# Where the third batch's quad 1 gets its norms: in the attention of the batch before, or amid the GELUs of the second w_in stage

## The chip, the cores and the metric

The kernel runs on one core of a Trainium2 chip. The metric is the device time of one execution in microseconds (us); "time" below is the median of several executions. A core has five engines that run in parallel, each strictly through its own list of instructions: TensorE (PE) multiplies matrices, ScalarE (ACT) evaluates functions such as exp and GELU, VectorE (DVE) and GpSimd (POOL) do elementwise work and sums, and SyncE (SP) issues transfers. They wait for each other through semaphores. PE writes its results to PSUM, [...]and an engine has to read a bank out before PE may write it again.

## The reference

Two steps in a row. First an attention with cosine scores over 8 batches of 12 heads, 448 positions and head dimension 64:

```python
q_n = q / (np.linalg.norm(q, axis=-1, keepdims=True) + 1e-06)
k_n = k / (np.linalg.norm(k, axis=-1, keepdims=True) + 1e-06)
scores = np.matmul(q_n, k_n.transpose(0, 1, 3, 2)) / tau
attn = softmax(scores)                     # max subtracted, exp, divided by the sum
attn_out = np.matmul(attn, v)
```

Then a feed-forward layer on x, the attention's output laid out as 3584 tokens of 768: `gelu_exact(x @ w_in) @ w_out`, with w_in 768 x 2048 and w_out 2048 x 768. Every row of q and k needs the root of its sum of squares before any score can be made; these norms are what the change is about.

## The kernel before

**Units of work.** Four heads make a quad; a batch has three quads, the kernel 24. A unit is a quad (quad 0 of the whole kernel is split into units 0 and 1), so quad g is unit g+1: the second batch (b = 1) has units 4, 5, 6, the third batch (b = 2) units 7, 8, 9, the fourth begins with unit 10.

**The norms of a unit** take this chain: `load_qk` (SP; q and k, 448 KB each), `square` (POOL, L156, 128x1792), `reduce` (DVE, L165, the sum of squares), `logs` (ACT, Ln, L172), `roots` (ACT, Exp of half the logarithm, L181), `inverses` (POOL adds 1e-6, L190; DVE reciprocal, L192), `scale` (POOL, twice, L208, writes bf16), `transposes` (SP, a transposing transfer, L220). `groups` says which units share one call of the three middle steps (`logs`, `roots`, `inverses`); the third batch's units 7 and 8 form one group, units 9 and 10 the next.

**The attention of a quad**: `scores` (PE, L246) into a pair of PSUM banks, `exps` (ACT, L253) from there, seven passes per quad; `both` then makes the row sums (PE, L275, tile `sm`), turns and inverts them on DVE (L297 to L318), multiplies by the values (PE, L289) and normalises (DVE, L323) into x.

**The stages.** For each batch b: `attention(b, fill)`, then `first(b)`, the w_in stage. The second matrix product (w_out, L352) of earlier tokens is cut into single matmuls, the list `fill`, that are dealt out between the attention's passes by `run()`; after each 16 of them DVE copies the finished bank out (tile `ot`, L356). A w_in stage is 16 blocks m of six matmuls each (L655), every block followed by one GELU on ACT (L691). ACT holds one table of functions at a time: a table load (L647, L693, L695, L700) comes before GELUs and before exps or logarithms.

**PSUM.** Two single banks, `mm0` and `mm1`, are handed out in turn by `mm_tile`; the row sums take the one whose turn it is. Three pairs, `st0`, `st1`, `st2`, serve scores and values. In `first(b)` with b of 1 or more,

```python
pairs = {2: 0, 4: 1} if b else {0: 1, 2: 0, 6: 1, 8: 0}
ahead = 6 if b else 5
```

so blocks 2 and 3 lie in `st0`, blocks 4 and 5 in `st1`, and blocks 0, 1, 6, 7, 8, ... 15 alternate over the two single banks: block 6 takes block 0's bank, block 7 takes block 1's, block 8 takes block 6's. In the first stage (b = 0) blocks 0, 1, 6, 7 lie in `st1`, blocks 2, 3, 8, 9 in `st0`, and the single banks hold blocks 4, 5 and then 10 to 15. The first `ahead` blocks are begun with four of their six matmuls, and finished with the last two once x is complete.

**The order** of every engine's list is the order of the calls in the program (a manual schedule). `upto(f, n)` calls step f for all units before n that have not had it. The first w_in stage already has a break amid its GELUs: after block 5 it loads the exp table, takes the roots of group 5 (units 5 and 6) and loads the GELU table again (L692 to L698).

Of the kernel before, what the change touches and what calls it, by code (L numbers as in the profile page):

```python
# [16 lines left out]
def kernel(  # L17
# [20 lines left out]
    NQ = H // 4  # L38
# [60 lines left out]
    def mm_tile(name, shape=(128, 512), dtype=F32, aside=None):  # L99
        t = ps_mm.tile(list(shape), dtype, tag=f"mm{turn[0] if aside is None else turn[0] ^ aside}", name=name)  # L100
        if aside is None:
            turn[0] ^= 1
        return t

    def pair(i, name):
        pool = third[0] if i == 2 else ps_st
        return pool.tile([128, 2, 512], F32, tag=f"st{i}", name=name)
# [3 lines left out]

    units = [(0, 0, 1), (0, 1, 2)] + [(g, 0, 2) for g in range(1, NG)]
    NU = len(units)
    groups = [[n] for n in range(NQ + 2)] + [[NQ + 2, NQ + 3], [2 * NQ + 1, 2 * NQ + 2]]
    for n in range(3 * NQ, NU, NQ):
        groups += [[n, n + 1], [n + 2]] if n + 2 < NU else [[n]]
    shapes = [[len(gr), 2, units[gr[0]][2] - units[gr[0]][1], C] for gr in groups]
# [51 lines left out]
    def logs(n):  # L169
        nq = nq_t.pop(n)  # L170
        ln_t[n] = nrm.tile(list(nq.shape), F32, tag="lq", name=f"lq{n}")
        nc.scalar.activation(ln_t[n], nq, AF.Ln, bias=tiny)  # L172

    def roots(n):
        ln = ln_t.pop(n)
        if n <= NQ:
            sr_t[n] = root2[n % len(root2)][:, :math.prod(shapes[n])]
            nc.scalar.activation(sr_t[n][:, :, 0], ln.rearrange("p j i s c -> p (j i s c)"), AF.Exp, scale=0.5)
        else:
            sr_t[n] = nrm.tile(list(ln.shape), F32, tag="sr", name=f"sr{n}")  # L180
            nc.scalar.activation(sr_t[n], ln, AF.Exp, scale=0.5)  # L181

    def inverses(n):
        sr = sr_t.pop(n)
        shape = [128] + shapes[n]
        se = nrm.tile(shape, F32, tag="se", name=f"se{n}")
        if n <= NQ:
            nc.vector.tensor_reduce(se.rearrange("p j i s c -> p (j i s c)"), sr, mybir.AxisListType.X, ALU.add)
        else:
            nc.gpsimd.tensor_scalar(se, sr, 1e-6, None, ALU.add)  # L190
        rn = nrm.tile(shape, F32, tag="rn", name=f"rn{n}")
        nc.vector.reciprocal(rn, se)  # L192
        rn_t[n] = rn
# [20 lines left out]
    def transposes(u, i=None):  # L214
        g, s0, s1 = units[u]
        qkb = qkb_t[g]
        if g not in qkT_t:
            qkT_t[g] = qkTp.tile([128, 2, C, 128], BF16, tag="qkT", name=f"qkT{g}")
        if i is None:
            nc.sync.dma_start_transpose(out=qkT_t[g].rearrange("p i c s -> p (i c) s"),  # L220
                                        in_=qkb.rearrange("p i c s d -> p (i c s d)"))
            return
        tp = tp_t[u, i] = mm_tile(f"tp{u}_{i}", (128, C, 128), BF16)
        for c in range(C):
            nc.tensor.transpose(tp[64 * s0:64 * s1, c, :], qkb[:, i, c, s0:s1].rearrange("p s d -> p (s d)"), ident)  # L225

    def copies(u, i):
        g, s0, s1 = units[u]
        rows = slice(64 * s0, 64 * s1)
        nc.vector.tensor_copy(qkT_t[g][rows, i], tp_t.pop((u, i))[rows])  # L230
# [94 lines left out]
    def both(g, p):  # L325
        sums(g)
        turned(g)
        inverted(g)
        spread(g, 0)
        spread(g, 1)  # L330
        values(g, p=p)
        normalise(g, 0)
        normalise(g, 1)
# [64 lines left out]
    def upto(f, n, last=None):  # L398
        last = {load_qk: NG, load_v: NV, root: len(groups), load_wi: 4, load_wo: 4}.get(f, NU)
        while done.get(f, 0) < min(n, last):  # L400
            done[f] = done.get(f, 0) + 1
            f(done[f] - 1)
# [180 lines left out]
    def visit(b, pairs):  # L583
        for p in pairs:
            n, c = passes[at.get(b, 0)]
            at[b] = at.get(b, 0) + 1
            scores(b * NQ + n, ((0, c), (1, c)), p)
            exps(b * NQ + n, ((0, c), (1, c)))

    def attention(b, fill):  # L590
        fill = list(fill)
        if len(fill) == 128:
            parts = iter((20, 18, 20, 22, 32, 16))
        else:
            parts = iter((20, 13, 14, 17, 16, 16) if b == 1 else (16, 14, 16, 18, 16, 16))

        def run():
            for _ in range(next(parts)):
                fill.pop(0)()

        x_t[b] = xp.tile([128, KD, S], BF16, tag="x", name=f"x{b}")
        g0, u = b * NQ, b * NQ + 1
        run()
        upto(scale, u + 3)
        upto(transposes, u + 3)
        if b == 1:
            upto(load_qk, g0 + NQ + 2)
            upto(square, u + 4)
        visit(b, (0, 1, 2))
        if b > 1:  # L610
            upto(scale, u + 4)
            upto(transposes, u + 4)
        run()
        visit(b, (0, 1, 2))
        run()
        upto(load_qk, g0 + NQ + 3)
        visit(b, (0, 1) if b <= 2 else (0, 1, 2))
        upto(reduce, u + 4)
        upto(square, u + 5)
        run()  # L620
        visit(b, (0, 1, 2))
        both(g0, 0)
        upto(load_v, b + 3)
        upto(load_qk, g0 + NQ + 4)
        visit(b, (1, 2))
        upto(reduce, u + 5)
        run()
        visit(b, (1, 2, 0))
        both(g0 + 1, 1)
        visit(b, (2, 0))  # L630
        n = 2 * b + 4
        if n < len(groups):
            logs(n)
            roots(n)
        run()
        both(g0 + 2, 2)
        if n < len(groups):
            inverses(n)
            done[root] = n + 1
            if b > 1:  # L640
                visit(b + 1, (0, 1))

    def first(b):
        sb, hf = divmod(b, 2)
        if hf == 0:
            g_t[sb] = gp.tile([128, KF, 2 * S], BF16, tag="g", name=f"g{sb}")
        nc.scalar.preload_act_table_set(GELU_SET)  # L647
        u = (b + 1) * NQ + 1
        hps = {}
        pairs = {2: 0, 4: 1} if b else {0: 1, 2: 0, 6: 1, 8: 0}  # L650
        ahead = 6 if b else 5

        def mm(m, kds):
            for kd in kds:
                nc.tensor.matmul(hps[m], lhsT=wi[:, kd, m * 128:(m + 1) * 128],  # L655
                                 rhs=x_t[b][:, kd, :], start=(kd == 0), stop=(kd == KD - 1))

        def bank(m):
            if m in pairs:
                st = pair(pairs[m], f"hp{b}_{m}")  # L660
                hps[m], hps[m + 1] = st[:, 0, :S], st[:, 1, :S]
            elif m not in hps:
                hps[m] = mm_tile(f"hp{b}_{m}")[:, :S]

        for m in range(ahead):
            bank(m)
            mm(m, range(KD - 2))
        if b == 0:
            upto(square, u + 3)
            upto(scale, u + 1)  # L670
            upto(transposes, u + 1)
            upto(load_wo, 4)
            upto(reduce, u + 3)
        else:
            upto(scale, u + 2)
            upto(transposes, u + 2)
            upto(load_qk, (b + 1) * NQ + 5)
            upto(square, u + 4)
            upto(reduce, u + 4)
        for m in range(ahead):  # L680
            mm(m, range(KD - 2, KD))
        for m in range(KF):
            if b == 0 and m == 8:
                for i in range(2):
                    transposes(4, i)
                    copies(4, i)
            if m >= ahead and (m == 0 or m - 1 not in pairs):
                for k in range(m, m + 1 + (m in pairs)):
                    bank(k)
                    mm(k, range(KD))  # L690
            nc.scalar.activation(g_t[sb][:, m, hf * S:(hf + 1) * S], hps.pop(m), AF.Gelu)  # L691
            if b == 0 and m == 5:  # L692
                nc.scalar.preload_act_table_set(EXP_SET)  # L693
                upto(root, 6)
                nc.scalar.preload_act_table_set(GELU_SET)  # L695
                upto(scale, u + 2)
                upto(transposes, u + 2)
                upto(load_qk, 2 * NQ + 1)  # L698
        if b + 1 < B:
            nc.scalar.preload_act_table_set(EXP_SET)  # L700
            if b <= 1:
                visit(b + 1, (0, 1, 2))
            upto(root, 2 * b + 6)

    upto(load_qk, 1)
    nc.scalar.preload_act_table_set(EXP_SET)
# [3 lines left out]
    late = nrm.tile([128, 1], F32, tag="late", name="late", bufs=1)  # L710
# [56 lines left out]
```

## Time and profile before

| what | value |
|---|---|
| median of 5 runs | 415.63 us (415.43 to 415.67) |
| the profiled execution: its time / its span | 415.63 us / 413.9 us |
| busy share of the span: PE, ACT, DVE, POOL | 98%, 59%, 46%, 40% |
| second attention, b = 1 (PE) | 52.1 to 80.7 us |
| second w_in stage, b = 1 (PE) | 80.7 to 99.0 us |
| third attention, b = 2 (PE) | 99.0 to 132.4 us |

The span is what the profiler saw from first to last instruction; 1.7 us of the execution's time lie around it. A line of the timeline gives the start, the duration, the engine, the line of the kernel, the operation, output and inputs, and in brackets how long the engine had been idle and who released it. A line of the chain gives the start, the duration, and the engine and tile of one piece of the work that ended last. "x5" counts instructions that the answer merged.

### The profile page before, as it was taken

Reading aid. Unit: us, or ns where it says so; the run is one execution under the profiler, and the core shown is the slowest. Engines: PE = TensorE matmul, PEld = TensorE weight load, DVE = VectorE, ACT = ScalarE, POOL = GpSimd, SP = SyncE. Lnnn points to the kernel's source line nnn. Section 1 sums busy time; section 2 is a strip of 40 time slices with the busy share of each in tenths; the row PEclk is TensorE's granted clock in tenths of the full one; section 3 lists DMA queues with packets and bytes.
Section 4 is the critical chain, followed back from the end, with each engine's and each line's share of the span. In section 5 each row is a group of like instructions: output and inputs, shape, how many; then the busy total and the mean of one; then the engine's idle time right before and its main releaser. Section 6 shows DMA issues by size and latency. Waiting matters only on the chain.

```text
span 413.9 us, 8268 instructions
## 1 busy us (share of the span) xinstructions
PE 406.9 (98%) x3506; PEld 212.4 (51%) x3506; DVE 188.4 (46%) x379; ACT 246.1 (59%) x358; POOL 166.9 (40%) x113
## 2 busy tenths in 40 slices
PE   7999999999999999999999999999999999999996
PEld 3445554555555555555555555555555555555564
DVE  5787216913278222943148431783118711481021
ACT  6895695546646567754764658755665467754300
POOL 4999706083810919044630537217370233000000
PEclk9999999999999999999999999999999999999999
DMA  8999998834396405935296332965088120510033
GB/s 290 261 261 206 204 227 274 185 66 115 62 226 200 122 13 91 280 93 123 25 209 216 66 107 46 219 188 133 2 171 190 40 44 2 120 40 2 0 78 77
DMA packets 66996, 54.53 MB, mean 132 GB/s; under 512 B 38672, under 2 KB 62352, under 8 KB 66960
## 3 DMA queue, kind: packets, MB, share of 16 engines
q1 hardware_dynamic: 54464, 41.79, 39.1%
q0 software_dynamic: 12112, 11.80, 18.1%
q8 instruction: 27, 0.44, 0.4%
q10 hardware_dynamic: 384, 0.43, 0.3%
q14 instruction: 9, 0.07, 0.1%
HBM read 45.61 MB, written 11.01 MB: 137 GB/s over the span
## 4 chain that ended last, share of the span: by engine, by line
PE 94%; DMA 2%; ACT 1%; DVE 1%; POOL 1%; issue 0%; SPq 0%; POOLq 0%
PE hp L655 35%; PE op L352 32%; PE st L246 9%; PE o L289 8%; PE sm L275 4%; PE spin L407 2%; DMA qk<-in_k_dram 2%; PE op L371 1%; PE sm L266 1%; PE tp L225 1%; ACT pt L253 1%; POOL sq L156 1%; DVE nq L165 0%; DVE qkT L230 0%; ACT g L691 0%
## 5 line engine op out<-in xcount | busy, mean ns | idle before, releaser
L253 ACT ACTIVATE pt<-st 128x896 bf16<-128x896 f32 x168 | 142.9, 917 | 67.2 <-PE st L246 66.9
L352 PE MATMUL op<-wo,g 128*128 128x384 bf16 x864 | 147.8, 326 | 0.0
L655 PE MATMUL hp<-x,wi 128*128 128x448 bf16 x768 | 146.8, 353 | 0.0
L352 PEld LDWEIGHTS <-g 128*128 128x128 bf16 x864 | 81.5, 98 | 62.3 <-issue 10.9
L655 PEld LDWEIGHTS <-wi 128*128 128x128 bf16 x768 | 74.4, 98 | 71.4 <-issue 2.9
L691 ACT ACTIVATE g<-hp 128x448 bf16<-128x448 f32 x128 | 65.9, 545 | 70.8 <-PE hp L655 70.5
L208 POOL TENSOR_TENSOR qkb<-qk,rn 128x896 bf16<-128x896 f32 (+1 forms) x49 | 79.6, 1649 | 40.5 <-DVE rn L192 40.5
L165 DVE TENSOR_REDUCE nq<-sq 128x28 f32<-128x1792 f32 (+2 forms) x30 | 48.8, 1637 | 58.0 <-POOL sq L156 55.3
L356 DVE COPY ot<-op 128x384 f32<-128x384 f32 x54 | 29.5, 548 | 95.5 <-PE op L352 93.4
L156 POOL TENSOR_TENSOR sq<-qk 128x1792 f32<-128x1792 f32 (+1 forms) x22 | 66.5, 3035 | 13.3 <-DMA qk<-in_k_dram 13.3
L190 POOL TENSOR_SCALAR se<-sr 128x28 f32<-128x28 f32 (+1 forms) x14 | 4.3, 309 | 125.5 <-ACT sr L181 125.4
L246 PE MATMUL st<-qkT 64*64 64x448 bf16 x672 | 47.8, 358 | 0.2 <-DVE qkT L230 0.2
L289 PE MATMUL o<-pt,v 64*64 64x448 bf16 x672 | 36.9, 352 | 0.0
L246 PEld LDWEIGHTS <-qkT 64*64 64x64 bf16 x672 | 18.3, 105 | 23.8 <-issue 15.4
L318 DVE STREAM_TRANSPOSE rs<-rc 128x448 f32<-128x448 f32 x48 | 28.1, 623 | 0.8
L323 DVE TENSOR_TENSOR x<-o,rs 128x448 bf16<-128x448 f32 x48 | 27.0, 599 | 1.0 <-DVE rs L318 0.5
L192 DVE RECIPROCAL rn<-se 128x28 f32<-128x28 f32 (+2 forms) x18 | 6.8, 376 | 43.4 <-POOL se L190 43.2
L289 PEld LDWEIGHTS <-v 64*64 64x64 bf16 x672 | 17.7, 106 | 16.9 <-issue 8.4
L297 DVE STREAM_TRANSPOSE tr<-sm 128x448 f32<-128x448 f32 x24 | 15.5, 647 | 13.8 <-PE sm L275 10.7
L275 PE MATMUL sm<-pt,ones 128*32 128x448 bf16 (+1 forms) x336 | 17.8, 332 | 0.7 <-DVE ot L356 0.7
L309 DVE TENSOR_REDUCE tr<-tr 32x28 f32<-32x28 f32 x84 | 16.5, 196 | 1.6
L407 PE MATMUL spin<-blank,ident 128*128 128x448 bf16 x34 | 10.3, 449 | 2.2 <-DVE root L89 1.9
(43 smaller groups left out, 115.5 us busy)
## 6 DMA issues: line engine op xcount, KB each, us to landing
qk<-in_q_dram SPq DMA_DIRECT2D x23, 448.0 KB, 6.2
qk<-in_k_dram SPq DMA_DIRECT2D x23, 448.0 KB, 8.6
out_dram<-ot SPq DMA_DIRECT2D x48, 192.0 KB, 3.4
v<-in_v_dram POOLq DMA_DIRECT2D x7, 672.0 KB, 12.4
wi<-in_moe_w_in_dram POOLq DMA_DIRECT2D x8, 384.0 KB, 13.3
wo<-in_moe_w_out_dram POOLq DMA_DIRECT2D x4, 768.0 KB, 13.7
out_dram<-ot SPq DMA_DIRECT2D x12, 96.0 KB, 2.2
qk<-in_q_dram SPq DMA_DIRECT2D x2, 224.0 KB, 3.4
```

The costliest lines, as they stand in the source:

```text
L156: eng.tensor_tensor(sq[:, part], t[:, part], t[:, part], ALU.mult)
L165: nc.vector.tensor_reduce(nq[:, part], sq[:, part], mybir.AxisListType.X, ALU.add)
L208: eng.tensor_tensor(qkb[:, i, :, s0:s1].rearrange("p c s d -> p s c d"), t[:, i, s0:s1], rn[:, i].to_broadcast([128, s1 - s0, C, D]), ALU. ...
L246: nc.tensor.matmul(st[cols, n, :S], lhsT=qkT[rows, 1, c, cols], rhs=qkT[rows, 0, :, cols], start=True, stop=True, tile_position=(64 * s, 6 ...
L253: nc.scalar.activation(pt[:, :m], st[:, :m, :S], AF.Exp, scale=inv_tau)
L275: nc.tensor.matmul(bank_t[g, "sm"][r:r + 32, cols], lhsT=ones, rhs=pt_t[g, s, c][:, cols], start=(c < 2), stop=(c >= C - 2), tile_position ...
L289: nc.tensor.matmul(bank_t[g, h][cols, :S], lhsT=v_t[g][rows, s, c, :], rhs=pt_t[g, s, c][rows], start=(c == 0), stop=(c == C - 1), tile_po ...
L318: nc.vector.transpose(rs, bank_t[g, "rc"][:, h].to_broadcast([128, NB, 32]))
L352: nc.tensor.matmul(ps[:, :NH], lhsT=g_t[sb][:, kf, t * 128:(t + 1) * 128], rhs=wo[:, kf, ni * NH:(ni + 1) * NH], start=(kf == 0), stop=(kf ...
L356: nc.vector.tensor_copy(ot[:, ni * NH:(ni + 1) * NH], ps[:, :NH])
L655: nc.tensor.matmul(hps[m], lhsT=wi[:, kd, m * 128:(m + 1) * 128], rhs=x_t[b][:, kd, :], start=(kd == 0), stop=(kd == KD - 1))
L691: nc.scalar.activation(g_t[sb][:, m, hf * S:(hf + 1) * S], hps.pop(m), AF.Gelu)
```

## The change

All of it is about the third batch's units 7 and 8 (quads 0 and 1), in the second attention and the second w_in stage.

- Units 7 and 8 each become a group of their own; the later groups' numbers move up by one, which the new `(b > 1)` and `(b > 0)` terms follow.
- In `attention(1)` the sum of squares of unit 7 moves from between the second `run()`s to after `both(g0, 0)`, that is behind the normalisation of quad 0 of the second batch, where the sum of unit 8 stood. The sum of unit 8 leaves the attention.
- At the end of `attention(1)`, `logs`, `roots` and `inverses` take unit 7 alone.
- In `first(1)`, ahead of the last two matmuls of the opening blocks, only unit 7 is scaled and transposed, only unit 9 is squared, and the sum of unit 8 stands there.
- In `first(1)`, after the GELU of block 5: exp table, roots of unit 8, GELU table, then scale and transpose of unit 8, square of unit 10 and the sums of units 9 and 10.

```diff
-    groups = [[n] for n in range(NQ + 2)] + [[NQ + 2, NQ + 3], [2 * NQ + 1, 2 * NQ + 2]]
+    groups = [[n] for n in range(NQ + 2)] + [[NQ + 2, NQ + 3], [2 * NQ + 1], [2 * NQ + 2]]
...
         visit(b, (0, 1) if b <= 2 else (0, 1, 2))
-        upto(reduce, u + 4)
         upto(square, u + 5)
...
         visit(b, (1, 2))
-        upto(reduce, u + 5)
+        upto(reduce, u + 4 + (b > 1))
...
-        n = 2 * b + 4
+        n = 2 * b + 4 + (b > 1)
...
-            upto(scale, u + 2)
-            upto(transposes, u + 2)
+            late = int(b == 1)
+            upto(scale, u + 2 - late)
+            upto(transposes, u + 2 - late)
             upto(load_qk, (b + 1) * NQ + 5)
-            upto(square, u + 4)
-            upto(reduce, u + 4)
+            upto(square, u + 4 - late)
+            upto(reduce, u + 4 - 2 * late)
...
-            if b == 0 and m == 5:
+            if b <= 1 and m == 5:
                 nc.scalar.preload_act_table_set(EXP_SET)
-                upto(root, 6)
+                upto(root, 6 if b == 0 else 8)
                 nc.scalar.preload_act_table_set(GELU_SET)
                 upto(scale, u + 2)
                 upto(transposes, u + 2)
-                upto(load_qk, 2 * NQ + 1)
+                if b == 0:
+                    upto(load_qk, 2 * NQ + 1)
+                else:
+                    upto(square, u + 4)
+                    upto(reduce, u + 4)
...
-            upto(root, 2 * b + 6)
+            upto(root, 2 * b + 6 + (b > 0))
```

## The prediction

> **What bounds the kernel now.** I read the page's busy shares first, then the chain that ended last in order of time, then the waits of PE, and then the timelines of the two places that the diff touches. The busy shares:
>
> ```profile
> PE 406.9 (98%) x3506; PEld 212.4 (51%) x3506; DVE 188.4 (46%) x379; ACT 246.1 (59%) x358; POOL 166.9 (40%) x113
> ```
>
> PE is the bound, so only what opens or closes a gap on PE counts. The chain shows one stretch after the start in which PE does not carry it:
>
> ```profile
> 52.17 0.55 ACT g L691
> 52.88 8.32 DMA qk<-in_k_dram
> 61.32 3.18 POOL sq L156
> 64.53 2.02 DVE nq L165
> 66.55 0.48 DVE ot L356
> 67.07 0.85 PE sm L275 x16
> ...
> 80.78 18.27 PE hp L655 x96
> ```
>
> From 67.07 to the copy that closes the run at 410 every piece is PE. The waits of PE between 30 and 110 us are a single entry:
>
> ```profile
> PE sm L275 <- DVE ot L356: 0.7, 1, 0.7
> ```
>
> The timeline there:
>
> ```profile
> 64.53 2.02 DVE L165 TENSOR_REDUCE nq<-sq 128x28 f32<-128x1792 f32 x1 [4.88 <-POOL sq L156]
> 65.59 0.76 PE L246 MATMUL st<-qkT 64*64 64x448 bf16 x12
> 66.47 1.01 DVE L356 COPY ot<-op 128x384 f32<-128x384 f32 x2
> 67.07 0.85 PE L275 MATMUL sm<-pt,ones 128*32 128x448 bf16 x16 [0.71 <-DVE ot L356]
> ```
>
> The sum of squares of unit 7 stands at the head of DVE's list from about 59.7 and waits 4.88 us for POOL's square, which waited for k to land. Behind it is queued the copy that empties the single bank the row sums want. Both copies run at 66.47 and PE has stood for 0.71 us. That gap is all that the first part of the change can win.
>
> The second place is the w_in stages. First stage, ACT, where the break amid the GELUs is already there:
>
> ```profile
> 37.77 2.81 ACT L691 ACTIVATE g<-hp 128x448 bf16<-128x448 f32 x6 [4.06 <-PE hp L655]
> 40.60 1.28 ACT L693 ACT_TABLE_LOAD   x1
> 42.07 0.34 ACT L172 ACTIVATE lq<-nq,tiny 128x56 f32<-128x56 f32 x1 [0.19 <-DVE nq L165]
> 42.45 0.25 ACT L181 ACTIVATE sr<-lq 128x56 f32<-128x56 f32 x1
> 42.71 1.28 ACT L695 ACT_TABLE_LOAD   x1
> 44.01 0.98 ACT L691 ACTIVATE g<-hp 128x448 bf16<-128x448 f32 x2
> ```
>
> From the end of the GELU of block 5 (37.77 + 2.81 = 40.58) to the start of block 6's GELU (44.01) the break takes 3.43 us, 0.19 of it a wait for DVE: 3.24 us without. PE has no wait in that stage. Second stage, PE and ACT, without a break:
>
> ```profile
> 80.71 18.33 PE L655 MATMUL hp<-x,wi 128*128 128x448 bf16 x96
> 86.97 2.43 ACT L691 ACTIVATE g<-hp 128x448 bf16<-128x448 f32 x5 [0.16 <-PE hp L655]
> 88.26 1.15 ACT L691 ACTIVATE g<-hp 128x448 bf16<-128x448 f32 x2
> 90.00 0.54 ACT L691 ACTIVATE g<-hp 128x448 bf16<-128x448 f32 x1 [0.59 <-PE hp L655]
> ```
>
> The second line holds blocks 2 to 6; the third is an answer for a narrower window and holds blocks 5 and 6. One GELU takes 0.54, so block 5's runs 88.26 to 88.80 and block 6's 88.87 to 89.41. The 96 matmuls start 0.189 apart (the first at 80.71, the last at 98.7: 18.0/95), so block 8, the 49th, starts at 80.71 + 48 x 0.189 = 89.8.
>
> **What the Trainium skill says.** (1) "ScalarE: Activation LUTs", section "What ACT_TABLE_LOAD costs", gives about 1283 ns for the load plus about 1380 ns of drain, about 2.66 us for a switch. The trace has the 1.28, and then the next instruction within 0.02 us (42.71 + 1.28 = 43.99, GELU at 44.01): no drain of that size here. I price with the trace; the skill's two switches would be 5.3 us. (2) Same page, section "Table sets: the hidden batching unit": logarithm and exp share a set, GELU has its own, so the break costs two loads, as the first stage shows. (3) "TensorE: Matmul & The Clock Gate", section "Part 1: The HAM clock gate": after one idle window of about 3.4 us the PE clock halves, and it takes one such window of work to come back. No run here shows it: the longest gap of PE in the middle is 0.71 us and the clock row of the page stands at 9 in all 40 slices.
>
> **The change, part by part.**
>
> *Unit 7's sum behind the normalisation.* The copy of the bank (its last matmul ends at about 63.0) no longer queues behind a stalled instruction and is over by 63.6; the row sums start when the scores leave PE, at 66.36. Next late is the third scores pair of the pass after: its exps end at 66.03 + 2.54 = 68.57, and PE would be there at about 68.5, so some 0.04 us stay (in the third attention the same place takes 0.42 us, here 0.38). Gain 0.71 - 0.04 = 0.67 us. DVE in the stretch 69.4 to 80.7 is busy 10.95 of 11.3 us, but it gets no second sum: unit 7's 2.0 us take the place of unit 8's 2.00 us at 72.25, with its square long done (64.5). Were the gain nil, because something else holds the row sums: 0; it cannot exceed 0.71.
>
> *Unit 8's sum in the w_in stage.* DVE is idle from 84.1 to 94.1 there; 2.0 us from 83.9 hide and end at 86, before the logarithm at 89. The copies of the later attention start at 104. Cost 0. Unit 7's logarithm, root, add and reciprocal at half width are 0.02 to 0.2 us shorter each, hidden as well.
>
> *The break in the second stage (times before the 0.67 shift).* ACT: block 5's GELU ends 88.80; load to 90.10; logarithm of 28 columns 0.32 and root 0.23, from start to start 0.35 to 0.41 (their pairs at 31.84/32.19 and 128.64/129.05), so the root ends at about 90.74; load to 92.03; block 6's GELU 92.05 to 92.59. Together 3.2 us in the place of 0.06. Queued behind it: the GELUs of 6 and 7. Who waits: block 8, which takes block 6's single bank and would start at 89.80. It starts 0.04 after the GELU's end, at 92.6. Stall on PE: 92.6 - 89.8 = 2.8 us. In the first stage the same break is free because blocks 6 to 9 lie in two pairs that blocks 0 to 3 have left, and the single banks come back only for block 10; in the second stage only blocks 6 and 7 have banks. The slack was 89.80 - 89.41 = 0.4 us; the break is eight times that. After it block 9 needs the GELU of 7 (ends by 93.1, PE wants it at 93.8) and block 10 that of 8, as before: no second stall. Bounds: 2.7 (shortest spacing) to 3.0 (a wait as the 0.19 above); the skill's drain would make it 4.9, which the trace excludes.
>
> *What moves on POOL, SP and DVE.* POOL: scale of unit 7 (2 x 1.66) from about 84, square of unit 9 (3.15) to 90.5, the add for unit 8 at about 91, its scale to 95, square of unit 10 to 98. DVE: reciprocal of unit 8 between, sums of 9 and 10 to 100.5 instead of 99.2; their logarithm was at 103.34 and goes to about 105.5 by the stall. SP: one transpose (about 2.4), then the load of quad 10, now some 3 us earlier, then unit 8's transpose behind the wait for its scale, about 95 to 98; nothing but stores and loads of the next attention is behind it, and those come after 103. Its result is first needed by scores at 106.86. Cover some 9 us; cost 0. Without cover it would be PE waiting by as much as it is late.
>
> *Sum.* -0.67 + 2.8 = +2.1 us on the profiled span: 413.9 to 416.0, and that execution's time 415.63, equal to the median of the runs, to 417.7. PE has no idle after 67.07 that could swallow the delay, so all of it reaches the end.
>
> **Rivals.**
>
> *A, the gain alone (other side).* The break hides as in the first stage, 415.63 - 0.67 = 414.96. This needs block 8 to have a bank other than block 6's, or the break to be shorter than 0.4 us; the kernel breaks even at a break of 0.4 + 0.67 = 1.1 us, and one table load alone is 1.28. For: the first stage does it without a wait. Against: the bank order in the second stage, which the diff leaves.
>
> *B, the clock.* PE stands 2.8 us, and the gate halves its clock for about one window: estimate from the skill's 3.4 us, half of it lost, +1.7: 419.4. Against: 2.8 is under the window. For: the margin is small and the trace shows no gap like it. From 3.4 us of idling it decides.
>
> *C, the gap at 66.4 stays* (the row sums held by exps or another copy): 415.63 + 2.8 = 418.4. Against: the exps of quad 3's passes are long done there, and the batch after has no gap in that place.
>
> *D, stalls partly met*: block 8's stall about half as large, because ACT's break starts earlier or overlaps, 416.4; or a further 0.5 to 1 us when block 9 or 10 waits again, 418.5.
>
> **How the numbers follow.** Main case 0.74 (417.3 to 418.2), A 0.05, B 0.09, C 0.05, D 0.07. Main, C and most of D give over 0.8 between 416.8 and 419.0; I take that as the range. Chances, with 0.2% (0.83 us) as about what a measurement of this kernel can tell from no change: faster only in A, and there 0.67 is just short of the bound, so 0.03; within 0.2%: the rest of A and a sliver of D, 0.04; slower 0.93.
>
> **What would show it.** Right: no wait of PE on an `ot` copy near 66.4; two further table loads at about 88; one wait of PE on ACT's GELU, 2.8 us long, in the second w_in stage at about 89.1; that stage 21.1 us long instead of 18.3; every later stage as long as before. Wrong: no wait there (A), matmuls spaced wider than 0.19 after it (B), a wait left near 66.4 (C).

## The result, and the profile after

The changed kernel takes 419.21 us (median of 43 executions, 417.34 to 421.63) against 415.66 us (median of 80) before. Compared side by side the ratio is 1.0077, 95% interval 1.0067 to 1.0086: slower by 2.8 to 3.6 us.

The profiled execution has a span of 416.9 us, 3.0 more than before. It began its first w_in stage at 32.53 us instead of 33.09, 0.56 us sooner in a part that the change leaves alone: at the start the matmuls are 0.373 us apart up to 5.59 us in this trace, up to 7.37 us in that of the kernel before, and 0.189 us from there on, so this execution came to its full speed earlier. Its second w_in stage began 1.27 us sooner (79.44 instead of 80.71) and is 4.31 us longer; together that is the 3.0. The medians lie 3.55 us apart (419.21 - 415.66).

The waits of PE in the changed kernel, columns as before (total us, times, longest):

```profile
PE hp L654 <- ACT g L691: 2.7, 1, 2.7
```

The wait of the row sums on the copy `ot` is gone from the list, and this one is new. The timeline where the old wait was:

```profile
62.58 0.56 DVE L356 COPY ot<-op 128x384 f32<-128x384 f32 x1 [3.49 <-PE op L352]
65.18 0.56 DVE L356 COPY ot<-op 128x384 f32<-128x384 f32 x1 [2.04 <-PE op L352]
65.77 0.85 PE L275 MATMUL sm<-pt,ones 128*32 128x448 bf16 x16
...
70.96 2.00 DVE L165 TENSOR_REDUCE nq<-sq 128x28 f32<-128x1792 f32 x1
```

The two copies run when their matmuls end, the row sums start without a bracket (no wait), and unit 7's sum runs behind the normalisation. In the chain the row sums start at 65.84 instead of 67.07; 0.56 of these 1.23 us is the earlier start, and the other 0.67 is the gain over an execution that starts like the profiled one of the kernel before. (With the sum in its old place an earlier start would not have brought the row sums forward: they wait for a transfer there, as experiment 4 shows.)

The second w_in stage, ACT and PE:

```profile
85.71 1.85 ACT L691 ACTIVATE g<-hp 128x448 bf16<-128x448 f32 x4 [0.16 <-PE hp L654]
87.58 1.28 ACT L693 ACT_TABLE_LOAD   x1
88.87 0.32 ACT L172 ACTIVATE lq<-nq,tiny 128x28 f32<-128x28 f32 x1
89.28 0.23 ACT L181 ACTIVATE sr<-lq 128x28 f32<-128x28 f32 x1
89.53 1.28 ACT L695 ACT_TABLE_LOAD   x1
90.82 0.98 ACT L691 ACTIVATE g<-hp 128x448 bf16<-128x448 f32 x2
91.42 10.66 PE L654 MATMUL hp<-x,wi 128*128 128x448 bf16 x48 [2.72 <-ACT g L691]
```

Block 5's GELU ends at 87.56, block 6's starts at 90.82: a break of 3.26 us. Block 8 starts 0.05 us after block 6's GELU (90.82 + 0.55 = 91.37). And the 48 matmuls from block 8 on take 10.66 us; the same 48 take 9.24 at full clock (experiment 1 below). The table by stretch says why. Its columns are the stretch, its length, busy us (and instructions) of PE, PE's weight loads, DVE, ACT and POOL, then the granted PE clock, the DMA share and GB/s:

```profile
79.44:88.70 9.26, 9.26 (x52) 4.71 (x49) 5.04 (x9) 3.95 (x7) 5.85 (x3) 1.00 0.32 69
88.70:90.92 2.22, 0.00 (x0) 0.00 (x0) 1.01 (x2) 2.09 (x5) 1.49 (x3) 1.00 1.00 193
90.92:94.34 3.42, 2.92 (x8) 1.13 (x8) 1.19 (x1) 1.37 (x3) 3.42 (x3) 0.50 0.52 200
94.37:102.01 7.64, 7.64 (x42) 3.80 (x40) 2.02 (x1) 3.28 (x7) 2.41 (x1) 1.00 0.32 60
```

PE is idle from 88.70; at 90.92, with 0.50 us of the idling still to come, the granted clock goes to one half, stays there for 3.42 us and comes back. Row by row the stage is 22.57 us long (79.44 to 102.01) instead of 18.26: 2.89 us from start to start by the stall (block 8 due 9.09 us after the stage's first matmul, as in the kernel before, that is at 88.53, and started at 91.42), 1.42 us by the clock.

The 43 executions fall into two kinds. 34 list a mean granted clock of 0.992 to 0.996 and take 418.66 us or more; nine list 0.998 or more, and seven of these take 417.34 to 417.94; the other two take 418.64 and 419.37, for a reason that no trace shows. A mean of 0.998 or 0.999 still means a clock that is whole as long as PE works: in the three kept traces that list one (experiments 4, 6 and 7) it halves only in the last 1.5 us, after the last matmul. So the clock falls amid the work in about four executions of five.

### The profile page after: what moved, and what is told of

Same layout as the page of the kernel before. It is cut to its first block, busy times and chain, and to the rows that moved or that the text cites. A ratio compares the mean times of both kernels' runs of the same rounds, so it can differ in the third digit from the quotient of the medians.

```text
span 416.9 us, 8274 instructions
## 1 busy us (share of the span) xinstructions
PE 407.7 (98%) x3506; PEld 212.5 (51%) x3506; DVE 188.6 (45%) x380; ACT 249.0 (60%) x362; POOL 167.2 (40%) x114
## 4 chain that ended last, share of the span: by engine, by line
PE 95%; ACT 2%; DVE 1%; DMA 1%; POOL 0%; issue 0%; DVEq 0%; ACTq 0%
PE hp L654 35%; PE op L352 35%; PE st L246 9%; PE o L289 8%; PE sm L275 4%; PE op L371 1%; PE sm L266 1%; PE tp L225 1%; DMA qk<-in_q_dram 1%; ACT g L691 1%; PE spin L407 0%; ACT pt L253 0%; POOL qkb L208 0%; ACT L695 0%; ACT L693 0%; DVE qkT L230 0%
## 5 line engine op out<-in xcount | busy, mean ns | idle before, releaser
L654 PE MATMUL hp<-x,wi 128*128 128x448 bf16 x768 | 148.4, 355 | 2.7 <-ACT g L691 2.7
L275 PEld LDWEIGHTS <-ones 128*32 128x32 bf16 x336 | 6.8, 96 | 9.0 <-issue 7.2
```

The source lines that it names most:

```text
L275: nc.tensor.matmul(bank_t[g, "sm"][r:r + 32, cols], lhsT=ones, rhs=pt_t[g, s, c][:, cols], start=(c < 2), stop=(c >= C - 2), tile_position ...
```

## The experiments

The medians of the kernel before on the same chip were 415.61 us for experiments 1, 2, 3 and 5, 415.78 for 4, 6 and 7, and 415.65 for 8 and 9.

**1. The stall without the idling.** The changed kernel, with matmuls on constants into the third pair of banks, which is free at that point, ahead of block 8:

```diff
         for m in range(KF):
+            if b == 1 and m == 8:
+                warm = pair(2, "warm")
+                for _ in range(13):
+                    nc.tensor.matmul(warm[:, 0, :S], lhsT=ident, rhs=blank, start=True, stop=True)
```

> The changed kernel with 13 extra matmuls on PE (12 x 0.19 = 2.3 us and one more) ahead of block 8 of the second w_in stage, into a pair of banks that is free there; nothing else differs, and block 8 still waits for the GELU of block 6. Theory 1 (the stall and a clock that halves because PE stood idle): the stall's place stays, the clock stays whole, all 96 matmuls 0.19 us apart; time 415.66 - 0.67 + 2.7 = 417.7 us, granted clock 0.999 or 1.0 in every execution, 1.5 us below the changed kernel. Theory 2 (the slow matmuls after block 8 have another cause than idling, such as the transfers or POOL work of those microseconds): they stay slow, 419.2 us.

Measured: 417.37 us (417.33 to 417.70), granted clock 1.0 in all five executions; ratio to before 1.0040 (1.0025 to 1.0056). The timeline of PE:

```profile
88.85 2.62 PE L690 MATMUL warm<-blank,ident 128*128 128x448 bf16 x13
91.73 9.24 PE L654 MATMUL hp<-x,wi 128*128 128x448 bf16 x48 [0.26 <-ACT g L695]
```

Block 8 waits for the same GELU as long as before, only 0.26 us of it idle, and the 48 matmuls take 9.24 us. The transfers and POOL's work of those microseconds are nearly the same (221 GB/s and 2.16 us busy, against 230 and 1.99 in the changed kernel), so the second theory falls: what slows the matmuls is that PE stood idle. 419.21 - 417.37 = 1.8 us of the change's loss is the clock; by the two ratios to the kernel before it is 1.5 us.

**2. Other banks for the second stage.**

```diff
         pairs = {2: 0, 4: 1} if b else {0: 1, 2: 0, 6: 1, 8: 0}
+        if b == 1:
+            pairs = {0: 1, 2: 0, 6: 1, 8: 0, 10: 2}
```

> The changed kernel, with the second w_in stage's blocks laid out over all three pairs: 0 and 1 and later 6 and 7 in one, 2 and 3 and later 8 and 9 in another, 10 and 11 in the third; the two single banks hold 4, 5, 12 to 15. Theory 1 (block 8 stalls only because it takes the bank of block 6, whose GELU stands behind the break): no wait of PE in the stage, no drop of the clock, stage 18.3 us; time 415.66 - 0.7 = 414.95 us. Theory 2 (the break overloads ACT, whichever bank is used): PE waits for later blocks, 1 us or more left, 416 us or above.

Measured: 414.66 us (21 executions), ratio to before 0.9974 (0.9964 to 0.9985). PE in that stage, and ACT's break:

```profile
79.80 18.33 PE L656 MATMUL hp<-x,wi 128*128 128x448 bf16 x96
...
88.05 1.28 ACT L695 ACT_TABLE_LOAD   x1
...
90.00 1.28 ACT L697 ACT_TABLE_LOAD   x1
91.30 1.85 ACT L693 ACTIVATE g<-hp 128x448 bf16<-128x448 f32 x4
```

The break is there with both loads and ACT's GELUs run late by as much, but the 96 matmuls are one piece of 18.33 us, as in the kernel before, without a wait. So the break costs PE only through the bank of block 6. This kernel computes the whole reference and beats both, the one before by 415.61 - 414.66 = 0.95 us. Its distance to experiment 1, 417.37 - 414.66 = 2.71 us, is the stall at full clock.

**3. The moved sum alone**, in the kernel before:

```diff
         visit(b, (0, 1) if b <= 2 else (0, 1, 2))
-        upto(reduce, u + 4)
         upto(square, u + 5)
...
-        upto(reduce, u + 5)
+        upto(reduce, u + 4 + (b > 1))
+        if b == 1:
+            nc.gpsimd.memset(nq_t[6][:, 1], 1.0)
+            done[reduce] = u + 5
```

> The kernel before, with one part of the change alone: the sum of squares of unit 7 stands behind the normalisation of quad 0, where unit 8's stood. Unit 8's sum is left out (a constant takes its place in the group's logarithm), so the output is not the reference's. Theory 1: only the 0.71 us wait of the row sums goes, 415.66 - 0.67 = 415.0 us. Theory 2 (the row sums are then held by something else): 415.66 us. If moving the sum starts a new wait: above 415.7.

Measured: 414.83 us (22 executions), ratio 0.9980 (0.9973 to 0.9987), that is -0.8 us; no wait of PE is left in that attention. Unit 8's sum is missing here, which takes 2 us from DVE; that this isn't what brings the gain is shown by experiment 2, which has every sum and gains 0.95 us. The size is a little above the 0.71 of one trace, though its interval (0.5 to 1.1 us) includes that; experiment 4 shows why more is possible.

**4. The break alone**: the changed kernel with unit 7's sum back in its old place.

```diff
         visit(b, (0, 1) if b <= 2 else (0, 1, 2))
+        upto(reduce, u + 4)
         upto(square, u + 5)
```

> The changed kernel with unit 7's sum of squares put back where the kernel before has it; the break amid the GELUs stays. If the two parts simply add, the row sums wait again (0.7 us or a little more, by when k lands), and the break costs what it costs in the changed kernel: 419.2 + 0.75 = 420.0 us, about 418.1 us in an execution whose clock stays whole. If the parts interact, it differs from 420.0 by more than 0.5 us.

Measured: 419.84 us (six executions). Two with a granted clock of 0.999 took 418.29 and 418.35; one with 0.998 took 421.63, which the clock doesn't explain. The waits of PE:

```profile
PE hp L655 <- ACT g L692: 2.7, 1, 2.7
...
PE sm L275 <- DVE ot L356: 1.2, 1, 1.2
```

The two parts add. The row sums' wait is 1.2 us in this trace and 0.7 in that of the kernel before. It begins when PE arrives and ends, by way of the square and the sum, with a transfer of k; both times differ from execution to execution. Of the five kept traces with unit 7's sum in its old place (this one, the kernel before and experiments 5 to 7) four show 1.2 us.

The profiled execution kept its clock, with the stall of the changed kernel. Its stretches around the stall, columns as above:

```profile
87.80:91.22 3.42, 1.92 (x11) 0.88 (x9) 0.29 (x2) 3.28 (x6) 2.83 (x2) 1.00 0.88 149
91.22:94.63 3.41, 2.19 (x12) 1.17 (x12) 1.92 (x2) 2.14 (x4) 3.29 (x2) 1.00 0.71 254
```

PE idles for 1.5 us of the first and 1.2 us of the second. Why they are cut at 91.22 is told under experiment 7.

**5 to 7. Idling of a chosen length.** The kernel before, with n idle GELUs after block 5 in the second stage, no table load:

```diff
+            if b == 1 and m == 5:
+                idle = consts.tile([128, S], BF16, name="idle")
+                for _ in range(5):
+                    nc.scalar.activation(idle, blank, AF.Gelu)
```

Five of them:

> The kernel before, with five more GELUs over a block of zeros, into a tile nobody reads, after the GELU of block 5 in the second w_in stage: a break of about 5 x 0.45 = 2.25 us without any table load. Stall of PE at block 8: 2.25 - 0.4 = 1.85 us. Theory 1 (the clock is judged over fixed windows of 3.4 us and halves when about half of one is idle; where the window falls is chance): in about half of the executions the time is 415.66 + 1.85 = 417.5 us at full clock, in the others about 1.5 us more. Theory 2 (the clock halves about 2.25 us after PE stopped): never, always 417.5 us. Theory 3 (table loads are what matters): no stall, 415.7 us.

Measured: 418.93 us (six executions). Three list a clock of 0.994 to 0.996 and take 419.47 to 419.71; three list 0.999 or 1.0 and take 417.98 to 418.39. The stretches of the profiled one:

```profile
80.65:89.90 9.25, 9.25 (x52) 4.71 (x49) 3.33 (x8) 3.90 (x9) 5.67 (x4) 1.00 0.29 66
89.90:92.14 2.24, 0.01 (x1) 0.00 (x0) 0.00 (x0) 2.18 (x5) 2.24 (x2) 1.00 0.57 108
92.14:93.40 1.26, 1.26 (x7) 0.68 (x7) 0.00 (x0) 0.39 (x1) 1.26 (x1) 1.00 1.12 214
93.40:96.82 3.42, 3.42 (x11) 1.32 (x9) 2.02 (x1) 1.09 (x2) 3.42 (x2) 0.50 1.01 280
```

The stall is 2.24 us, not 1.85: the idle GELUs do not overlap and start 0.61 us apart, where the stage's own GELUs start 0.42 us apart. The clock falls 1.26 us after PE has gone back to work, 3.5 us after it stopped. That excludes a limit counted from the moment PE stops (theory 2), and the table loads as the cause (theory 3).

Four of them:

> The kernel before with four idle GELUs (each 0.59 us from start to start, as with five) after block 5: stall at block 8 about 2.24 - 0.59 = 1.65 us. Theory 1 (fixed windows of 3.4 us, the clock halves when half of one, 1.7 us, is idle): the clock never falls, 415.6 + 1.65 = 417.3 us. Theory 2 (any idle of over 1 us inside one window is enough): it falls in most executions, and the median is 1.5 us higher, 418.8 us.

Measured: 417.78 us (seven executions), stall 1.62 us in the trace. Five list 0.999 or 1.0, as theory 1 has it; one lists 0.996 (418.90) and one 0.992 (420.01), which it doesn't explain. Those two left no trace that could show where their clock fell.

Seven of them:

> The same with seven idle GELUs: stall about 2.24 + 1.18 = 3.4 us, a whole window long. Theory 1: however the windows fall, one of them is at least half idle, so the clock falls in every execution; 415.6 + 3.4 + 1.5 = 420.5 us, up to 422 where a second window is lost. Theory 2: the same. If executions at full clock (419.0 us) are left, half a window is not the bound.

Measured: 420.46 us (six executions). Four list 0.991 to 0.995 and take 420.37 to 421.82. Two keep their clock (0.998 and 1.0; 419.73 and 419.11), the profiled one among them:

```profile
90.45:93.91 3.46, 0.01 (x2) 0.00 (x1) 0.00 (x0) 3.33 (x7) 3.46 (x2) 1.00 0.76 146
93.91:103.08 9.17, 9.17 (x50) 4.59 (x49) 4.04 (x2) 4.19 (x8) 3.77 (x2) 1.00 0.44 121
```

PE idles for 3.46 us and the clock stays whole. So half a window isn't the limit; it lies above. The trace's records of the granted clock (start and length in us, share of full speed) point to the reason:

```text
after      16.257   85.333  1.0     101.591   3.413  0.5     105.004  324.266  1.0     429.270  0.297  0.5
5 GELUs    15.154   88.747  1.0     103.901   3.413  0.5     107.314  320.853  1.0     428.167  2.264  0.5
7 GELUs    17.496  409.599  1.0     427.095   3.457  0.5
```

The last record of a row lies at the end of the execution. Every stretch at full clock is a whole number of 3.4133 us long (25 and 95, 26 and 94, and 120 times that), and so it is in the other eight kept traces. The clock changes only on the marks of a grid of 3.413 us that differs from execution to execution. The timeline begins at 10.669, 10.501 and 10.577 us of this count. So the changed kernel has a mark at 90.92, and the window between marks that ends there held 2.22 idle us; with five GELUs the window from 89.99 to 93.40 held 2.15. With seven GELUs a mark at 92.25 cuts the idling. The windows there (the first two lines), and the end of the same execution (the last two):

```profile
88.84:92.25 3.41, 1.62 (x9) 0.72 (x8) 0.00 (x0) 3.25 (x8) 3.41 (x3) 1.00 0.70 135
92.25:95.67 3.42, 1.76 (x10) 0.94 (x10) 1.09 (x1) 2.44 (x5) 3.42 (x2) 1.00 0.95 162
...
413.10:416.52 3.42, 1.32 (x20) 1.11 (x18) 0.72 (x2) 0.00 (x0) 0.00 (x0) 1.00 0.45 115
416.52:417.96 1.44, 0.00 (x0) 0.00 (x0) 0.00 (x0) 0.00 (x0) 0.00 (x0) 0.50 0.00 0
```

The end of the changed kernel:

```profile
411.77:415.19 3.42, 1.58 (x23) 1.35 (x20) 0.71 (x2) 0.00 (x0) 0.00 (x0) 1.00 0.45 111
415.19:416.88 1.69, 0.00 (x0) 0.00 (x0) 0.00 (x0) 0.00 (x0) 0.00 (x0) 1.00 0.06 14
```

Windows with 1.8 and 1.7 idle us leave the clock whole, and so does the one with 3.42 - 1.58 = 1.84; after the one with 3.42 - 1.32 = 2.10 it halves. So 2.10 idle us in one window were enough, and 1.84 were not. From the first record of the clock on, every window of the eleven kept traces agrees, that of experiment 4 too, where the mark at 91.22 cuts a stall of 2.7 us into 1.5 and 1.2.

An estimate tests this on the executions without a trace. If the marks lie anywhere with equal chance and the limit is L, a stall of length I leaves a share of (2L - I) / 3.413 with a whole clock. With L from 1.84 to 2.10 that is 0.28 to 0.43 for 2.72 us, 0.42 to 0.57 for 2.24 and 0.06 to 0.22 for 3.46; the lists have 9 of 43, 3 of 6 and 2 of 6. The order of size is right, and more can't be told from so few.

**8 and 9. The limit, tried on the changed kernel.** Experiment 1 with 6 matmuls in place of 13, and the changed kernel itself beside it.

```diff
-                for _ in range(13):
+                for _ in range(6):
```

> The changed kernel with 6 extra matmuls in place of 13 ahead of block 8: they shorten the time that PE idles there from 2.72 to about 1.6 us, and block 8 starts as late as before. If the clock falls once about 1.8 to 2.1 us of one fixed window of 3.4 us are idle, it never falls here, and the time is that of 13 matmuls, 417.4 us. If PE has to be busy nearly all the time, or less idling is enough, part of the executions lies 1.5 us higher.

> The changed kernel itself, beside it on the same chip: most executions near 419.2 us with a granted clock of 0.994 to 0.996, some near 417.4 with a whole clock. The difference of the two whole-clock levels is the stall alone, and should be nil.

Measured: with six matmuls 417.68 us (417.26 to 418.01), clock 0.999 or 1.0 in all five executions, and a wait of 1.58 us for the GELU in the trace. The changed kernel beside it: 418.83 us (six executions), four with 0.994 to 0.996 at 418.61 to 419.51, two with 0.999 at 417.31 and 417.71. Idling of 1.6 us in place of 2.7 takes the fall of the clock away, and the whole-clock levels agree.

## Why the prediction was right or wrong

The direction and the two terms of the sum hold; the likeliest time was too low, because a case that I had set aside is the common one.

- *Unit 7's sum behind the normalisation, -0.67.* Right: 0.67 in the trace, -0.8 us as a run of its own (experiment 3). I took the 0.71 us of one trace as the most it could give, and that was wrong: the wait varies with k's landing and PE's arrival, and four other traces have 1.2 us.
- *Unit 8's sum in the w_in stage, 0.* Right: it ran from 82.62 to 84.58, ahead of the logarithm at 88.87.
- *The break, +2.8.* Right: break 3.26 us for 3.2, start-to-start delay of block 8 2.89 us for 2.8, no second stall, and 2.71 us as the difference of experiments 1 and 2. "ScalarE: Activation LUTs" of the Trainium skill, section "What ACT_TABLE_LOAD costs", puts a drain of 1.4 us on top of each load; here 1.28 + 0.01 to 0.02 us was all. (The 4.9 us that I gave for the stall with the drain left out the logarithm and the root: as an estimate from that page it would be 3.2 + 2 x 1.38 - 0.4 = 5.6.)
- *What moves on POOL, SP and DVE, 0.* Right: unit 8's scale ended at 93.65 and its transpose was issued at 93.68, with its scores not due before 109.9; the logarithm of units 9 and 10 found its sums done at 98.8.
- *Rival A (the gain alone)*: not what the change does, but its condition, another bank for block 8, was right: experiment 2 gives 414.66 where the rival's sum gave 414.96.
- *Rival B, the clock.* This is the step that failed. I wrote that 2.8 is under the window and that "from 3.4 us of idling it decides", and gave it 0.09. The clock fell in 34 of 43 executions. I had read "TensorE: Matmul & The Clock Gate", section "Part 1: The HAM clock gate", as asking for a whole window of 3.4 us without work. The grid of 3.413 us is in the traces, but a window with 2.10 to 2.22 idle us was enough, so the measurement decides against that reading. The rival's time, 419.4, and its price of 1.7 us were close: 1.42 us in the trace after, where 0.50 us of the slow window was idle anyway, and 10.93 - 9.24 = 1.69 with five GELUs.

The main case, 417.7, is what seven of the nine executions with a whole clock take (417.34 to 417.94). The median of all, 419.21, lies just above the range's end of 419.0; by the side-by-side ratio the time is 415.66 x 1.0077 = 418.9. That this lies inside is luck: the range was drawn from the main case, C and D, all with a whole clock, and left the 419.4 of rival B out.

## What to carry to other kernels

Before a slow piece is put into an engine's list, look up which buffers wait behind it, not how busy the engine is: the same break of 3.2 us on ACT is free in a stage where the next blocks have four banks or more of their own, and costs PE 2.7 us where they have two. A stall of PE of about 2 us or more should be priced with the chance of one slow window on top: 1.4 to 1.7 us here, in 34 of 43 executions with 2.7 us and 3 of 6 with 2.2 us. Where the stall can't be avoided, a few matmuls on constants into a free bank removed that part, in all ten executions of experiments 1 and 8.

## What the runs showed of the hardware that I had not expected

The granted PE clock changed only on the marks of a grid of 3.4133 us, whose place differs from execution to execution. It was halved for one window when 2.10 us or more of the window before were idle, even where PE was back at work by then, and not when 1.84 us or less were. So an idle time of 3.46 us, which a mark cut into 1.8 and 1.7, did not halve it, and 2.24 us did. The changed kernel takes for the most part one of two times, about 417.5 or about 419.3 us, by where the marks fall in its stall.

The way up asks for a busier window than the way down. At the start of the kernel PE waits 1.93 us for its first matmul, and the marks cut this wait too: a window with 0.69 idle us brought the full clock (five GELUs), one with 1.22 us did not (experiment 3). The full clock came at 4.65 us in the one and at 7.53 in the other, and their first w_in stages began at 32.3 and 33.1 us.

Where the limit lies between 1.84 and 2.10 us stays open, and so does why two of seven executions with a stall of 1.6 us list a lower clock. A fall need not come from that stall: of the 66 executions of the kernel before that were measured beside the experiments, one lists 0.992.
